# First batch of an FFT-mixing and SwiGLU kernel: its copies on VectorE, its loads and stores on other queues, and products of zeros on TensorE while it waits

## The chip, the cores and the metric

One core of a Trainium2 chip. The metric is the device time of one launch in microseconds (us); a time quoted for a kernel is the median of its runs. Engines in the profile: PE is TensorE (matrix products), PEld its weight loads, DVE is VectorE, ACT ScalarE, POOL GpSimd, SP the engine that only issues transfers. "ACTq", "POOLq" and "SPq" are the queues on which those engines issue transfers.

## The reference

```python
def _attn_ref(x, filt_r, filt_i):                 # x: 8 x 3008 x 256
    X = np.fft.rfft(x, axis=1)
    Y = X * (filt_r + 1j * filt_i)[None, :, :]
    return np.fft.irfft(Y, n=x.shape[1], axis=1).astype(np.float32)

def _moe_ref(x, w_gate, w_val, w_out):            # x: 24064 x 256; w: 256 x 1536, 1536 x 256
    g = x @ w_gate
    silu = g * (1.0 / (1.0 + np.exp(-g)))
    return (silu * (x @ w_val) @ w_out).astype(np.float32)
# reference: the first, reshaped to (8 * 3008, 256), then the second
```

The weights arrive as 64-bit numbers, and the kernel rounds them to float32 on the chip ("rounding" below).

## The kernel before

The transform over 3008 = 47 x 64 points is done in steps of products with tables. For each batch: the first step (`pa`) multiplies x by a 94x96 table and stores the result in DRAM (`d1`); the second step loads it back turned (`t`), multiplies by the table `tb` (2a), multiplies by the filter `f` on VectorE (`p`, `q`), adds `p` and `q` on GpSimd, multiplies by the inverse table (2b, `pc`), and stores `g` in DRAM (`d2`); the third step loads that (`t4`) and multiplies by the last table (`pd`), which gives `y`, the input of the feed-forward part. Batches 1 to 7 are woven into the feed-forward products of the batch before them. Batch 0 has nothing to hide behind: it stands alone at the start of the program, and it is what the change edits.

Several functions serve all batches; `self.b` is the number of the batch. Cuts are marked.

```python
def load_weights(j):                       # raw 64-bit weights, all on SP's queue
    if j < len(weights):
        raws[j] = rpool.tile([128, 2, 2, 128, 2], U32, name=f"raw_{j}", tag="raw", bufs=2)
        for i in range(2):
            nc.sync.dma_start(out=raws[j][:, i], in_=weights[j][0][:, i])

def round_weights(j):                      # VectorE, ScalarE, then GpSimd
    load_weights(j + 2)
    # ... (cut)

def load_tables(self, parts=3):            # class Spectral, batch 0 only
    # ... (cut)
    for i in range(parts):
        nc.scalar.dma_start(out=tb[:, ts(i, n)], in_=de_dram[:, ts(i, n)])
        for rows, view in filter_parts():  # 4 of them: f_r twice, f_i twice
            nc.scalar.dma_start(out=f[rows, ts(i, n), :], in_=view(n * i, n))

def stage1(self, u):                       # 16 steps a batch
    # ... (cut)
    p1 = spool0 if self.b == 0 and u % 2 else t1pool      # batch 0: 2 + 2 buffers
    t1 = p1.tile([NK, NV, C], FP32, name=f"t1_{self.b}_{u}", tag="t1", bufs=2)
    ps = fps.tile([128, NV, C], FP32, name=f"pa_{self.b}_{u}", tag="f")
    nc.tensor.matmul(out=ps[0:NK], lhsT=wf_t, rhs=self.x.pop(u), start=True, stop=True)
    nc.scalar.copy(out=t1, in_=ps[0:NK])
    queue = nc.scalar if self.b == 1 else nc.gpsimd
    queue.dma_start(out=self.d1_rows[:, ts(u, NV), :], in_=t1)

def stage2a(self, u):                      # 12 steps a batch; loads t on SP's queue
    # ... (loads and the two products into ps: cut)
    for h in (lo, hi):
        nc.vector.tensor_tensor(out=pt[h], in0=ps[h], in1=fr, op=ALU.mult)
    nc.vector.scalar_tensor_tensor(out=qt[lo], in0=ps[hi], scalar=-1.0, in1=fi,
                                   op0=ALU.mult, op1=ALU.mult)
    nc.vector.tensor_tensor(out=qt[hi], in0=ps[lo], in1=fi, op=ALU.mult)
    add(nc.gpsimd, pt, pt, qt)

def stage2b(self, u):
    # ... (two products into ps: cut)
    nc.scalar.copy(out=g, in_=ps)
    for p in range(2):
        queue = nc.scalar if self.b == 0 and p else nc.gpsimd
        queue.dma_start(out=..., in_=g[64 * p:64 * p + 64])

# the start of the program
for i in range(4):
    spec.load_x(i)                         # SP's queue
spec.load_tables()                         # ScalarE's queue
load_weights(0)
load_weights(1)
nc.sync.dma_start(out=wi_t, in_=wi_dram.ap())
for u in range(N_ONE):
    spec.stage1(u)
for _ in range(2):
    round_weights(todo.pop(0))
lag = 3
for u in range(N_TWO + lag):
    if u < N_TWO:
        spec.stage2a(u)
    if u >= lag:
        spec.stage2b(u - lag)
for i in range(2):
    spec.load_t4(0, i)
for step in range(4):
    spec.stage3(0, step)                   # pd and y
```

A scheduler orders the instructions of each engine; only those marked with `keep_in_program_order` are kept as written.

Of the kernel before, what the change touches and what calls it, by code (L numbers as in the profile page):

```python
# [49 lines left out]
NK = 4 * NS  # L50
# [53 lines left out]
def kernel(  # L104
# [10 lines left out]
    nc = tc.nc  # L115
# [3 lines left out]
    de_dram = nc.inline_tensor(de_host, name="de_tbl").ap()  # L119
# [23 lines left out]
    wv_t = cpool.tile([128, NJ, 7, 128], FP32)  # L143
# [5 lines left out]
    def filter_parts():  # L149

        for k, filt in enumerate((filt_r, filt_i)):
            for half in range(2):
                off, step = (0, 1) if half == 0 else (N1, -1)

                def view(s0, n, filt=filt, off=off, step=step):
                    return bass.AP(tensor=filt.tensor, offset=filt.offset + (off + step * s0) * C,
                                   ap=[[N1 * C, 32], [step * C, n], [1, C]])

                yield slice(64 * k + 32 * half, 64 * k + 32 * half + 32), view

    def add(eng, dst, a, b):
        eng.tensor_tensor(out=dst, in0=a, in1=b, op=ALU.add)  # L162

    def sub(eng, dst, a, b):
        eng.tensor_tensor(out=dst, in0=a, in1=b, op=ALU.subtract)  # L165
# [3 lines left out]
    def weight_parts():  # L169

        cols = [w.bitcast(U32).rearrange("(a p) (h j f two) -> j p h a f two",
                                         a=2, p=128, h=2, j=NJ, two=2)
                for w in (moe_w_gate, moe_w_val)]
        rows = moe_w_out.bitcast(U32).rearrange("(l j p) (c f two) -> j p l c f two",
                                                l=2, j=NJ, p=128, c=2, two=2)
        def hid(j):
            for w, dst in zip(cols, (wg_t, wv_t)):
                yield w[j], dst[:, j], True

        for q in range(NQB):  # L180
            for j in range(JB * q, JB * q + JB):
                yield from hid(j)
            for j in range(JB * q, JB * q + JB):
                yield rows[j], wo_t[:, j], False

    weights = list(weight_parts())
    raws = {}

    def load_weights(j):
        if j < len(weights):  # L190
            raws[j] = rpool.tile([128, 2, 2, 128, 2], U32, name=f"raw_{j}", tag="raw", bufs=2)
            for i in range(2):
                nc.sync.dma_start(out=raws[j][:, i], in_=weights[j][0][:, i])

    def round_weights(j):



        load_weights(j + 2)
        raw, (_, dst, left) = raws.pop(j), weights[j]  # L200
        low, high = raw[:, :, :, :, 0], raw[:, :, :, :, 1]
        pw = rpool.tile([128, 2, 2, 128], U32, name=f"pw_{j}", tag="pw")
        w = rpool.tile([128, 2, 2, 128], FP32, name=f"w_{j}", tag="w")
        man = w.bitcast(U32)
        v = nc.vector
        flat = "p a b f -> p (a b f)"
        flat2 = "p a b f two -> p (a b f) two"

        pin = tc.keep_in_program_order
        pin(v.tensor_scalar(out=man, in0=high, scalar1=0xFFFFF, scalar2=None,  # L210
                            op0=ALU.bitwise_and))
        pin(nc.scalar.activation(out=w, in_=man, func=AF.Copy, scale=2.0 ** -20, bias=1.0))
        pin(v.tensor_scalar(out=pw, in0=high, scalar1=20, scalar2=0x7FF,
                            op0=ALU.logical_shift_right, op1=ALU.bitwise_and))
        pin(nc.scalar.activation(out=pw, in_=pw, func=AF.Relu, bias=off_t))
        v.tensor_scalar(out=pw, in0=pw, scalar1=255.0, scalar2=2.0 ** 23,
                        op0=ALU.min, op1=ALU.mult)
        v.scalar_tensor_tensor(out=pw.rearrange(flat), in0=raw.rearrange(flat2)[:, :, 1],
                               scalar=0x80000000, in1=pw.rearrange(flat),
                               op0=ALU.bitwise_and, op1=ALU.bitwise_or)  # L220
        v.scalar_tensor_tensor(out=w.rearrange(flat), in0=raw.rearrange(flat2)[:, :, 0],
                               scalar=2.0 ** -52, in1=w.rearrange(flat),
                               op0=ALU.mult, op1=ALU.add)

        e = nc.gpsimd
        pin(e.tensor_tensor(out=dst[:, 0:4, :].rearrange("p (a b) f -> p a b f", b=2), in0=w,
                            in1=pw.bitcast(FP32), op=ALU.mult))
        if left:
            a11, a12, a21, a22, s1, s2, s4 = [dst[:, i] for i in range(7)]
            add(e, s1, a21, a22)  # L230
            sub(e, s2, s1, a11)
            sub(e, a21, a11, a21)
            sub(e, s4, a12, s2)
        else:
            b11, b12, b21, b22, t1, t2, t4 = [dst[:, i] for i in range(7)]
            sub(e, t1, b12, b11)
            sub(e, t2, b22, t1)
            sub(e, b12, b22, b12)
            sub(e, t4, b21, t2)
# [2 lines left out]

    def bank(kind, name):
        return wps.tile([128, 512], FP32, name=f"w{kind}_{name}", tag=kind)

    class Spectral:

# [47 lines left out]
        def load_tables(self, parts=3):  # L295

            tb = spool0.tile([128, NS, 2, 128], FP32, name="tb0")
            f = spool0.tile([128, NS, C], FP32, name="f0")
            n = NS // parts
            for i in range(parts):  # L300
                nc.scalar.dma_start(out=tb[:, ts(i, n)], in_=de_dram[:, ts(i, n)])
                for rows, view in filter_parts():
                    nc.scalar.dma_start(out=f[rows, ts(i, n), :], in_=view(n * i, n))
            for u in range(N_TWO):
                self.tb[u], self.f[u] = tb[:, ts(u, NV)], f[:, ts(u, NV)]

# [4 lines left out]
        def stage1(self, u):  # L311

            if self.b:
                for v in (0, 1, 2) if u == 0 else (u + 2,):
                    self.load_x(v)
            p1 = spool0 if self.b == 0 and u % 2 else t1pool
            t1 = p1.tile([NK, NV, C], FP32, name=f"t1_{self.b}_{u}", tag="t1", bufs=2)
            ps = fps.tile([128, NV, C], FP32, name=f"pa_{self.b}_{u}", tag="f")
            nc.tensor.matmul(out=ps[0:NK], lhsT=wf_t, rhs=self.x.pop(u), start=True, stop=True)  # L319
            nc.scalar.copy(out=t1, in_=ps[0:NK])  # L320
            queue = nc.scalar if self.b == 1 else nc.gpsimd
            queue.dma_start(out=self.d1_rows[:, ts(u, NV), :], in_=t1)

# [31 lines left out]
        def stage2b(self, u):  # L355

            pt, tb = self.p.pop(u), self.tb.pop(u)
            ps = fps.tile([128, NV, C], FP32, name=f"pc_{self.b}_{u}", tag="f")
            for i in range(NV):
                nc.tensor.matmul(out=ps[:, i, :], lhsT=tb[:, i, 1, :], rhs=pt[:, i, :],  # L360
                                 start=True, stop=True)
            p3 = spool0 if self.b == 0 and u % 2 else gpool
            g = p3.tile([128, NV, C], FP32, name=f"g_{self.b}_{u}", tag="g", bufs=2)
            nc.scalar.copy(out=g, in_=ps)
            for p in range(2):
                a0 = p * NS + NV * u
                queue = nc.scalar if self.b == 0 and p else nc.gpsimd
                queue.dma_start(out=self.d2[a0:a0 + NV].rearrange("s n c -> n s c"),
                                in_=g[64 * p:64 * p + 64])

# [151 lines left out]
    todo = list(range(len(weights)))  # L522
# [7 lines left out]
    with tc.tile_pool(name="start", bufs=1) as spool0:  # L530
        for i in range(4):
            spec.load_x(i)
        spec.load_tables()
        load_weights(0)
        load_weights(1)
        nc.sync.dma_start(out=wi_t, in_=wi_dram.ap())
        for u in range(N_ONE):
            spec.stage1(u)
        for _ in range(2):
            round_weights(todo.pop(0))  # L540
        lag = 3
        for u in range(N_TWO + lag):
            if u < N_TWO:
                spec.stage2a(u)
            if u >= lag:
                spec.stage2b(u - lag)
    for i in range(2):
        spec.load_t4(0, i)
    for step in range(4):
        spec.stage3(0, step)  # L550
    for _ in range(2):
        round_weights(todo.pop(0))
# [10 lines left out]
    for b in range(B):  # L563
# [26 lines left out]
        for i in range(NP):  # L590
            k, j = divmod(i, NJ)
# [47 lines left out]
```

## Time and profile before

| | before |
|---|---|
| time, median of the first three runs | 3150.79 us (3150.08 to 3152.27) |
| first product of the second step (2a) starts | 77.33 us |
| VectorE's work of the second step | 79.41 to 118.15 us |
| third step (pd) starts | 133.18 us |
| last subtraction of the third step on VectorE starts | 139.42 us |

The prediction below shows the emptiest and the fullest stretches of the start. These are the ones between (columns: stretch, length, then busy us and instructions of PE, PEld, DVE, ACT, POOL, granted clock, share of the 16 DMA engines, GB/s):

```profile
40.00:60.00 20.00, 15.71 (x18) 4.92 (x19) 0.00 (x0) 7.00 (x11) 5.31 (x10) 1.00 0.69 178
60.00:80.00 20.00, 11.48 (x17) 4.66 (x16) 3.34 (x6) 5.94 (x10) 6.37 (x11) 1.00 0.50 148
100.00:120.00 20.00, 10.17 (x28) 6.36 (x28) 15.09 (x22) 3.51 (x6) 9.42 (x11) 0.67 0.27 69
```

The first step runs from 40 to 70 us, on TensorE and ScalarE, after the loads; VectorE has almost nothing to do until 70 us. From 100 us to the end of its second step at 118.15 us VectorE, which should be the bound there, is busy for 15 us of 18. The list of its waits from 55 to 125 us (total us, times, longest) has a line for that:

```profile
DVE q L349 <- POOL p L162: 3.3, 3, 2.1
```

It waits for GpSimd's sums `p + q`, and GpSimd stands in order behind stores of `g` that it issues itself. Last, what the DMA engines moved from 20 to 40 us, while no product could run:

```profile
DMA packets 2062, 4.49 MB, mean 225 GB/s; under 512 B 201, under 2 KB 1701, under 8 KB 1701
```

### The profile page before, as it was taken

To read this page: it belongs to the slowest core of one execution; us is meant where nothing else is said; L and a number is where in the kernel's file an instruction comes from. 1 tells how busy PE (TensorE), PEld (TensorE's weight loads), DVE (VectorE), ACT (ScalarE), POOL (GpSimd) and SP (SyncE) were. 2 spreads that over 40 slices of the span, in tenths; PEclk is the share of its full clock that TensorE was granted. 3 is DMA by queue.
4 is the path that set the end of the run, shared out by engine and by line. 5 is a ranking of instruction groups with operands and counts; after the bars stand their busy time and mean duration, and the time that the engine had idled before them with its cause. 6 is when DMAs were issued, how large, how long until landed. Compare 5 with 4: busy or idle time off the path is not lost.

```text
span 3150.0 us, 41042 instructions
## 1 busy us (share of the span) xinstructions
PE 3042.9 (97%) x15488; PEld 2236.8 (71%) x15488; DVE 1461.6 (46%) x2331; ACT 1149.9 (37%) x2086; POOL 1409.8 (45%) x1634
## 2 busy tenths in 40 slices
PE   3689999999999999999999999999999999999999
PEld 1456777677777777777777677777777677777776
DVE  0665544345533445335543455434554445544443
ACT  1244333433334333433334433333333433333333
POOL 1475554345543345434444445434544345533333
PEclk9799999999999999999999999999999999999999
DMA  8432322213222223122222222221321212210000
GB/s 191 113 119 88 87 64 61 70 54 90 68 57 63 71 64 87 50 70 64 77 60 60 67 81 67 62 65 54 87 74 52 71 55 77 64 31 21 21 5 17
DMA packets 122481, 212.50 MB, mean 67 GB/s; under 512 B 23670, under 2 KB 68214, under 8 KB 121426
## 3 DMA queue, kind: packets, MB, share of 16 engines
q1 hardware_dynamic: 91388, 128.58, 14.8%
q0 software_dynamic: 25024, 70.29, 7.7%
q10 hardware_dynamic: 5872, 11.01, 1.5%
q8 instruction: 122, 2.00, 0.3%
q14 instruction: 75, 0.61, 0.1%
HBM read 134.81 MB, written 74.97 MB: 67 GB/s over the span
## 4 chain that ended last, share of the span: by engine, by line
PE 80%; POOL 8%; DVE 5%; issue 3%; DMA 2%; ACT 2%; SPq 0%; POOLq 0%; ACTq 0%; DVEq 0%
PE wA_v L419 15%; PE wA_g L419 15%; PE wA_o L483 7%; PE wE_v L419 7%; PE wE_g L419 7%; PE wE_o L483 7%; PE wF_o L483 4%; PE wF_g L419 4%; PE pd L380 4%; PE wF_v L419 3%; PE pa L319 3%; POOL o L162 3%; POOL h L165 3%; PE pc L360 3%; PE pb L340 2%
## 5 line engine op out<-in xcount | busy, mean ns | idle before, releaser
L419 PE MATMUL wA_v<-y,wv_t 128*128 128x376 f32 x1536 | 613.8, 481 | 8.6 <-ACT u_v L428 6.5
L419 PE MATMUL wA_g<-y,wg_t 128*128 128x376 f32 x1536 | 615.7, 483 | 0.9 <-ACT u_g L428 0.9
L165 POOL TENSOR_TENSOR h<-h 128x376 f32<-128x376 f32 x576 | 567.1, 985 | 28.8
L162 POOL TENSOR_TENSOR h<-h 128x376 f32<-128x376 f32 x192 | 189.0, 984 | 705.9 <-PE wE_v L419 387.7
L428 ACT COPY u_g<-wA_g 128x376 f32<-128x376 f32 x576 | 269.5, 468 | 587.3 <-PE wA_g L419 585.0
L419 PEld LDWEIGHTS wA_v<-y,wv_t 128*128 128x128 f32 x1536 | 290.7, 191 | 205.8 <-DVE h L441 15.8
L483 PEld LDWEIGHTS wA_o<-wo_t,h 128*128 128x128 f32 x3456 | 407.5, 193 | 16.5 <-issue 0.6
L483 PE MATMUL wA_o<-wo_t,h 128*128 128x128 f32 x3456 | 418.7, 276 | 0.0
L419 PEld LDWEIGHTS wA_g<-y,wg_t 128*128 128x128 f32 x1536 | 282.1, 191 | 167.2 <-issue 28.0
L446 ACT ACTIVATE s<-s 128x1128 f32<-128x1128 f32 x192 | 219.5, 1143 | 375.9 <-DVE s L162 375.9
L448 DVE TENSOR_TENSOR h<-s,h 128x1128 f32<-128x1128 f32 x192 | 256.3, 1335 | 123.4 <-ACT s L446 123.2
L419 PE MATMUL wE_v<-y,wv_t 128*128 128x376 f32 x768 | 307.9, 483 | 3.4 <-DVE h L162 3.4
L419 PE MATMUL wE_g<-y,wg_t 128*128 128x376 f32 x768 | 306.3, 481 | 1.8 <-DVE s L162 1.2
L428 ACT COPY u_v<-wA_v 128x376 f32<-128x376 f32 x576 | 272.2, 473 | 69.9 <-PE wA_v L419 66.0
L162 DVE TENSOR_TENSOR s<-u_g,wE_g 128x376 f32<-128x376 f32 x384 | 209.0, 544 | 176.8 <-ACT u_g L428 174.9
L483 PE MATMUL wE_o<-wo_t,h 128*128 128x128 f32 x2304 | 282.1, 277 | 7.5 <-DVE o L162 7.5
L162 DVE TENSOR_TENSOR s<-u_g,wF_g 128x376 f32<-128x376 f32 x192 | 104.5, 544 | 393.7 <-PE wF_g L419 375.4
L483 PE MATMUL wF_o<-wo_t,h 128*128 128x128 f32 x2304 | 278.6, 275 | 0.0
L483 PEld LDWEIGHTS wE_o<-wo_t,h 128*128 128x128 f32 x2304 | 267.7, 192 | 14.1 <-DVE o L162 13.6
L483 PEld LDWEIGHTS wF_o<-wo_t,h 128*128 128x128 f32 x2304 | 267.8, 192 | 0.3
L162 DVE TENSOR_TENSOR h<-u_v,wE_v 128x376 f32<-128x376 f32 x384 | 209.1, 545 | 28.1 <-ACT u_v L428 5.1
L419 PEld LDWEIGHTS wE_v<-y,wv_t 128*128 128x128 f32 x768 | 146.3, 191 | 102.1 <-DVE h L162 5.1
(82 smaller groups left out, 3222.7 us busy)
## 6 DMA issues: line engine op xcount, KB each, us to landing
t<-d SPq DMA_DIRECT2D x192, 128.0 KB
t<-d SPq DMA_DIRECT2D x64, 384.0 KB
d<-g POOLq DMA_DIRECT2D x180, 128.0 KB, 2.8
d<-t POOLq DMA_DIRECT2D x112, 192.0 KB, 2.4
tb<-de_tbl SPq DMA_DIRECT2D x84, 256.0 KB
x<-in_x_dram SPq DMA_DIRECT2D x112, 160.0 KB
out_dram<-o POOLq DMA_DIRECT2D x128, 128.0 KB, 2.0
f<-in_filt_r_dram SPq DMA_DIRECT2D x168, 64.0 KB
```

What stands on the lines that cost most here:

```text
L162: eng.tensor_tensor(out=dst, in0=a, in1=b, op=ALU.add)
L165: eng.tensor_tensor(out=dst, in0=a, in1=b, op=ALU.subtract)
L319: nc.tensor.matmul(out=ps[0:NK], lhsT=wf_t, rhs=self.x.pop(u), start=True, stop=True)
L340: nc.tensor.matmul(out=ps[:, i, :], lhsT=self.tb[u][:, i, 0, :], rhs=t2[:, i, :], start=True, stop=True)
L360: nc.tensor.matmul(out=ps[:, i, :], lhsT=tb[:, i, 1, :], rhs=pt[:, i, :], start=True, stop=True)
L380: nc.tensor.matmul(out=psv[:, n, :], lhsT=self.t4[k, i][:, n, ts(cb, 128)], rhs=wi_t, start=True, stop=True)
L419: nc.tensor.matmul(out=bk[z][kind], lhsT=wt[z][:, j, LEFT[p], :], rhs=y[:, RIGHT[p], :], start=start, stop=True, skip_group_check=True)
L428: nc.scalar.copy(out=u[(1, 6, 7).index(p)], in_=bk[z]["A"])
L446: nc.scalar.activation(out=s[:, 0:3], in_=s[:, 0:3], func=AF.Silu)
L448: nc.vector.tensor_tensor(out=h[:, 0:3], in0=s[:, 0:3], in1=h[:, 0:3], op=ALU.mult)
L483: nc.tensor.matmul(out=bk[kind][:, t, :], lhsT=hs[i][:, HID[p], t0:t0 + 128], rhs=wo_t[:, JB * q + i, WO[p], :], start=start and t == 0 an ...
```

## The change

Its intent: let the first step follow x as it lands, instead of after all loads; take issue work off GpSimd in the second step; and keep TensorE's clock up through the waits with products of zeros ("fillers"). The core of the diff:

```diff
-    def load_weights(j):
+    def load_weights(j, queue=nc.sync):
...
-    def round_weights(j):
-        load_weights(j + 2)
+    def round_weights(j, following=True):
+        if following:
+            load_weights(j + 2)
...
+    def warm(count, width=4):
+        for i in range(count):
+            ps = bank("F", "idle")[:, 0:128 * width]
+            tc.keep_in_program_order(nc.tensor.matmul(
+                out=ps, lhsT=wv_t[:, 0, 0, :],
+                rhs=wv_t[:, 0, 0:width, :].rearrange("p i f -> p (i f)"), start=True, stop=True))
...  (load_tables)
-                nc.scalar.dma_start(out=tb[:, ts(i, n)], in_=de_dram[:, ts(i, n)])
+                nc.sync.dma_start(out=tb[:, ts(i, n)], in_=de_dram[:, ts(i, n)])
                 for rows, view in filter_parts():
-                    nc.scalar.dma_start(out=f[rows, ts(i, n), :], in_=view(n * i, n))
+                    queue = nc.scalar if rows.start >= 64 else nc.sync
+                    queue.dma_start(out=f[rows, ts(i, n), :], in_=view(n * i, n))
...  (stage1)
-            nc.scalar.copy(out=t1, in_=ps[0:NK])
+            if self.b:
+                nc.scalar.copy(out=t1, in_=ps[0:NK])
+            else:
+                nc.vector.tensor_copy(out=t1, in_=ps[0:NK])
...  (stage2b)
-                queue = nc.scalar if self.b == 0 and p else nc.gpsimd
+                queue = nc.gpsimd if self.b else nc.scalar
...  (the start of the program)
-        load_weights(0)
-        load_weights(1)
+        load_weights(0, nc.scalar)
+        load_weights(1, nc.scalar)
         nc.sync.dma_start(out=wi_t, in_=wi_dram.ap())
+        nc.vector.memset(wv_t[:, 0], 0.0)
+        warm(5)
         for u in range(N_ONE):
             spec.stage1(u)
+            warm(1, 2)
+        warm(6)
         for _ in range(2):
-            round_weights(todo.pop(0))
+            round_weights(todo.pop(0), False)
...  (after the second step)
+    for j in (2, 3):
+        load_weights(j)
     for i in range(2):
         spec.load_t4(0, i)
+    warm(9)
```

So raw weights 2 and 3 are now loaded after the second step, in program order, and not at the first two roundings.

More of the change, by code (lines that the diff above doesn't have):

```diff
@@ L192, in load_weights @@
             for i in range(2):
-                nc.sync.dma_start(out=raws[j][:, i], in_=weights[j][0][:, i])
-    def round_weights(j):
-        load_weights(j + 2)
+                ins = queue.dma_start(out=raws[j][:, i], in_=weights[j][0][:, i])
+                if j in (2, 3):
+                    tc.keep_in_program_order(ins)
+    def round_weights(j, following=True):
+        if following:
+            load_weights(j + 2)
         raw, (_, dst, left) = raws.pop(j), weights[j]
```

## The prediction

> **What bounds the kernel now.** I read the page first, then the table by stretches, then the chain of work over the first 145 us, then the waits there, and last the timeline and the DMA queues of the same stretch.
>
> ```profile
> PE 3042.9 (97%) x15488; PEld 2236.8 (71%) x15488; DVE 1461.6 (46%) x2331; ACT 1149.9 (37%) x2086; POOL 1409.8 (45%) x1634
> PE   3689999999999999999999999999999999999999
> ```
>
> From 280 us on TensorE is never idle, so only the start can give anything. (A slice is 78.75 us: the 3 and the 6 are the first 157 us.) The change edits the first batch only; with line and buffer numbers removed, the instructions of TensorE are the same in both kernels from about the 220th of 7782 on, and those of the other engines likewise after the start. I take the rest as shifted in time, not altered. By stretches (columns: PE, PEld, DVE, ACT, POOL busy, granted clock, DMA share, GB/s):
>
> ```profile
> 0.00:20.00 20.00, 3.98 (x4) 0.79 (x4) 0.06 (x1) 0.00 (x0) 0.20 (x4) 1.00 0.95 210
> 20.00:40.00 20.00, 0.00 (x0) 0.00 (x0) 0.76 (x2) 0.00 (x0) 0.00 (x0) 1.00 1.06 225
> 80.00:100.00 20.00, 14.14 (x56) 10.86 (x54) 18.91 (x30) 2.34 (x4) 11.84 (x15) 1.00 0.65 182
> 120.00:140.00 20.00, 10.60 (x40) 9.38 (x41) 1.31 (x2) 2.81 (x4) 4.44 (x6) 0.50 0.34 83
> ```
>
> For 40 us nothing computes and the DMA engines are full; then VectorE is the bound (18.91 of 20); then nothing is, in a tail at half the clock. The chain of waits says why (start, length, what):
>
> ```profile
> 11.36 18.38 DMA tb<-de_tbl
> 30.20 10.08 DMA raw<-in_moe_w_val_dram
> 40.66 1.28 ACT L320
> 42.84 7.88 DMA d<-t
> 51.43 17.40 PE pa L319 x20
> ...
> 73.70 3.50 DMA t<-d
> 77.33 2.06 PE wA_b L340 x4
> ...
> 133.18 7.11 PE pd L380 x32
> ```
>
> The first step's products (pa) had data at 11 us, but their copies stand on ScalarE behind 15 table loads that it issues itself, and the last of those gets into its queue at 40.6 us:
>
> ```profile
> ACT L320 <- DMA raw<-in_moe_w_val_dram: 40.7, 1, 40.7
> PE pa L319 <- ACT t L320: 28.1, 2, 26.4
> PE pd L380 <- DMA t<-d: 7.7, 1, 7.7
> ```
>
> After that pa runs at 1.71 us a step (timeline: 7.04 us for four steps). In the second batch two of its instructions take 0.88 to 1.02 us, so it runs at half speed here, although the granted clock of the page reads 1.00.
>
> **What the Trainium skill says.** "TensorE: Matmul & The Clock Gate", Part 1, states that the array runs at half clock until activity of about 3.4 us has been seen, and falls back after an idle window of that length. The trace agrees on the fall (pd 7.11 us for 32 instructions at 133 us, 1.76 for 16 at 229 us). It does not agree on the rise: 17.4 us of gapless pa products stay at half speed, while the full 128x128 products from 77 us on speed up within about 5 us. "TensorE: Matmul & The Clock Gate", Part 1, "Architectural detail", calls ScalarE a strict FIFO: the 40.7 us wait above is that. "DMA: Bandwidth & Descriptors", "Rules for kernel authors", says that spreading transfers over issuing engines gives no bandwidth, only issue time, as all run on the same 16 engines. The trace of 0 to 40 us agrees, the two queues' shares adding to one whole:
>
> ```profile
> q10 hardware_dynamic: 1583, 4.54, 51.8%
> q1 hardware_dynamic: 1795, 4.16, 48.9%
> ```
>
> **The change part by part.**
>
> *Start of the second step (2a).* The copies go to VectorE, which has nothing to do, so the first step can follow x as it lands. VectorE's 64x512 operations from PSUM take 0.69 us (timeline), so a copy of 96x512 costs about that, 16 of them 11 us beside the loads. But the transfers remain: x, tables and two raw weights together are 10.3 MB, which at the measured 218 GB/s is 47 us, and the trace shows the queues full until about 48 us. The first step's stores, 16 of 192 KB, ran alone from 50 to 70 us at 36 to 40% of the engines, so they need 10 us of all engines. In the old kernel these follow the loads; now they mix with them. As loads and stores share the engines, 47 + 10 = 57 us is the earliest that everything is done. The loads of the second step (t<-d) stand on the SP queue behind x, all of tb and half of f, the longest of the three queues, so I expect them at about 57 us, the first landing 3.5 us later (as at 73.70). First 2a product: 60.5 instead of 77.3: **16.8 us**. The five zero products before are about 7 us and end before x; the half-width ones between (0.43 us each at full speed) and the six after lie in the wait. They matter to the clock only.
>
> *Second step on VectorE.* From 79.41 to 118.15 it took 38.7 us. Its period per step where nothing else interferes is 2.83 us (p starts at 86.62, 89.44, 92.27, 95.10), so 12 steps need 33.9. The rest is 1.6 us of rounding the second weight and 3.3 us of waits for GpSimd's sums, which stood in order behind GpSimd's own stores of g. Rounding now falls in the wait before 2a, and all g stores go to ScalarE (a copy of 0.58 and two issues of about 0.6 us are under 2.83). So 38.7 becomes 34.1: **4.6 us**.
>
> *Tail.* From VectorE's end at 118.15 to pd at 133.18 are 15.0 us. Now: sum 1.3, two products 1.1 to 2.1, copy 0.6, issues 0.6, landing 2.6, t4 load 3.8, some 0.4 between: 10.4 to 11.4. Against it stand the nine filler products (by now with real weights, as the zeros are overwritten): 0.86 us each at full speed, 1.71 cold. If TensorE has cooled as before, two to four are slow and the nine take 9.4 to 11 us, while the transfers they cover take about 8. I count 11.8 us from VectorE's end to pd: **3.2 us**.
>
> *Third step.* pd at full speed is 2 x 1.76 = 3.5 instead of 7.1 us: **3.6 us**. Behind it, the products at 140 us run at 1.25 us a pair instead of 0.63, but they soon wait for rounded weights (weight product on TensorE at 152.9 waits for GpSimd), a chain that starts with VectorE after pd. So little more: **0.5 us**.
>
> Sum: 16.8 + 4.6 + 3.2 + 3.6 + 0.5 = 28.7 us. 3150.8 - 28.7 = **3122 us**.
>
> **The rivals.** *The tables do not bind; the first step does.* SP's packets are larger, so its queue may get more than its share and finish early; t<-d would then go as soon as the last store has landed, near 50 us. That the author placed only six filler products (5.2 us) after the first step speaks for it: about a store and a load. Against: all queues seem saturated until the sum is through. It would give 7 us more: 3115. *The queue order turns the gain into a new wait.* The SP queue alone, with few transfers admitted at a time, does not fill the engines, or stores under full load take as long as the one at 42.84 (7.88 us), four buffers at a time, which stretches the first step. 2a would start near 68: 3130. From 40 to 45 us one queue alone held 98% of the engines, which speaks against the first half. *The fillers are too long.* Cold, nine take 15.4 us, delaying pd by 4 to 5 us against my count: 3127. *The gain is swallowed later*, because from 140 to 245 us weight rounding, not TensorE, sets the pace (GpSimd busy 17.89 of 20 us from 160 on). But that work starts relative to pd and its loads wait on buffers, not on a fixed time, so it moves along; if half were lost, 3136.
>
> **Range and chances.** The start of 2a is the widest term (52 to 67 us), the tail and the fillers plus or minus 3. I predict **3122 us**, 3113 to 3132 eight times in ten. Two per cent is 63 us. To win it the whole start would have to shrink from 140 to 77 us, less than the 57 us of transfers and the 34 us of VectorE work in series; to lose it needs a fault that nothing here hints at. Faster 0.01, same 0.98, slower 0.01.
>
> **What would show each step.** In the changed profile: the first pa copy on VectorE before 15 us; DMA shares near 1 to about 57 us with all three queues in it; the first 2a product at 60.5; VectorE's second step 34 us long, without waits for GpSimd; pd beginning 11 to 12 us after it and lasting 3.5 us; the same spacing from pd to the steady state, about 29 us earlier. I am wrong if 2a starts at 52 or 68, if the fillers end well after t4 has landed, or if the lead at 150 us is not the lead at the end.

## The result, and the profile after

| | before | after | earlier by |
|---|---|---|---|
| time, median of four runs | 3151.23 us | 3118.31 us | 32.9 us |
| first 2a product | 77.33 | 55.09 | 22.2 us |
| VectorE's second step | 79.41 to 118.15 (38.7 long) | 57.07 to 90.95 (33.9 long) | 27.2 us at its end |
| pd starts | 133.18 | 102.99 | 30.2 us |
| last subtraction of the third step | 139.42 | 108.43 | 31.0 us |
| span of the profiled run | 3150.0 | 3116.7 | 33.3 us |

The ratio of the times is 0.9898, with a 95% interval of 0.9881 to 0.9915. By the 2% rule the two kernels count as the same; the interval still excludes 1.

The page of the kernel after, totals and TensorE's slices:

```profile
PE 3056.4 (98%) x15560; PEld 2240.5 (72%) x15560; DVE 1476.5 (47%) x2348; ACT 1140.3 (37%) x2070; POOL 1405.8 (45%) x1622
PE   7789999999999999999999999999999999999999
```

TensorE is busier by 13.5 us than before, and the program is shorter: the fillers fill idle time. The first three slices (78 us each) read 7, 7, 8 where they read 3, 6, 8. A busy TensorE in the first slice is therefore no sign of progress here. The stretches say more (columns as before):

```profile
0.00:20.00 20.00, 15.50 (x34) 6.97 (x34) 3.61 (x6) 1.28 (x1) 2.44 (x8) 1.00 0.96 200
20.00:40.00 20.00, 13.69 (x33) 6.48 (x33) 6.18 (x9) 0.00 (x0) 4.10 (x8) 0.83 1.03 331
40.00:60.00 20.00, 16.24 (x35) 8.87 (x36) 10.54 (x18) 2.56 (x4) 9.03 (x15) 0.74 0.69 217
60.00:80.00 20.00, 15.29 (x63) 10.83 (x61) 19.50 (x29) 4.04 (x7) 8.98 (x8) 1.00 0.64 172
```

VectorE works from the first stretch on (the copies), and from 60 to 80 us it is the bound of the second step, at 19.50 of 20. The DMA engines are full to 40 us as before, yet they moved 331 GB/s where they had moved 225. The chain of waits (start, length, what) shows what sets each part:

```profile
15.21 10.54 DMA d<-t
...
33.70 7.52 DMA d<-t
...
45.09 6.15 DMA d<-t
...
55.34 2.42 DMA t<-d
...
92.44 2.08 PE pc L376 x4
94.51 8.64 PE wF_idle L254 x18
103.15 0.88 PE pd L396 x8
104.06 0.82 ACT y L407
104.92 0.90 PE wA_g L435 x2
105.82 1.77 PE pd L396 x16
```

Where table loads and a copy on ScalarE stood, there are now the landings of the first step's stores (`d<-t`, 6 to 10 us each): eight of the sixteen copies waited for one of the four buffers to come free, 18.0 us in total. After 94 us the fillers (`wF_idle`) stand on the path, and within pd a product of the feed-forward part (`wA_g`) that waited 0.91 us for a copy on ScalarE. SP's waits up to 60 us name what the second step's loads waited for:

```profile
SPq L304 <- DMA d<-t: 7.8, 3, 6.3
```

The loads of `t` were issued at 51.38 us, when the last store had landed. The DMA engines from 20 to 40 us, the counterpart of the line with the 4.49 MB:

```profile
DMA packets 2316, 6.62 MB, mean 331 GB/s; under 512 B 334, under 2 KB 1415, under 8 KB 1872
q1 hardware_dynamic: 863, 3.93, 60.0%
q0 software_dynamic: 611, 1.87, 29.4%
q10 hardware_dynamic: 842, 0.81, 14.1%
```

Queue q0 is GpSimd's and carries the first step's stores; q1 is SP's and q10 ScalarE's, and both carry loads alone in this stretch. The loads make 3.93 + 0.81 = 4.74 MB, no less than the 4.49 MB of before. The 1.87 MB of stores came on top. Over all of the first 48 us the change moved 10.37 MB of loads and 2.70 MB of stores, the kernel before 10.39 and 0.12.

### The profile page after: what moved, and what is told of

Its sections match the earlier page's. It is cut to its first block, busy times and chain, and to the rows that moved or that the text cites. A ratio compares the mean times of both kernels' runs of the same rounds, so it can differ in the third digit from the quotient of the medians.

```text
span 3116.7 us, 41163 instructions
## 1 busy us (share of the span) xinstructions
PE 3056.4 (98%) x15560; PEld 2240.5 (72%) x15560; DVE 1476.5 (47%) x2348; ACT 1140.3 (37%) x2070; POOL 1405.8 (45%) x1622
## 4 chain that ended last, share of the span: by engine, by line
PE 80%; POOL 7%; DVE 6%; issue 3%; DMA 2%; ACT 2%; SPq 0%; POOLq 0%; ACTq 0%; DVEq 0%
PE wA_v L435 15%; PE wA_g L435 15%; PE wA_o L499 7%; PE wE_v L435 7%; PE wE_g L435 7%; PE wE_o L499 7%; PE wF_o L499 4%; PE wF_g L435 4%; PE pd L396 3%; PE wF_v L435 3%; POOL o L162 3%; PE pa L332 3%; POOL h L165 3%; PE pc L376 2%; PE pb L356 2%
## 5 line engine op out<-in xcount | busy, mean ns | idle before, releaser
L162 POOL TENSOR_TENSOR p<-p,q 128x512 f32<-128x512 f32 x96 | 121.6, 1266 | 226.4 <-DVE q L367 226.4
```

The costliest lines, as they stand in the source:

```text
L162: eng.tensor_tensor(out=dst, in0=a, in1=b, op=ALU.add)
```

## The experiments

Theories before the first run. Main theory: the gain is the copies (the first step runs beside the loads), then the queues of `g`, and the fillers give next to nothing. Rival: the fillers' clock gives several us. On the start of 2a there were two more: the landing of the stores through four buffers sets it, or the amount of transfers queued ahead of the loads of `t` does. The kernels ran in three groups, each with its own runs of the kernel before, whose medians were 3148.96 us (the first four kernels below), 3151.91 (the next four) and 3151.28 (the last four); so ratios are compared across groups, and times within one; each group ran on another chip.

### 1. The change without its fillers

```diff
-        warm(5)
-            warm(1, 2)
-        warm(6)
-    warm(9)
```

> The changed kernel without any filler product. Theory A (the second step starts when the last store of the first step has landed; the first step is paced by those landings through four buffers of t; the fillers only serve the clock of the third step): first 2a product at 55 to 57 us, VectorE's second step 34 us, pd at half clock, 7 us long; total 3119 to 3123. Rival C (the fillers carry a good part of the gain, by keeping the first and second steps at full clock): 2a at 60 or later, or a longer second step; total 3126 or more.

Measured: 3119.88 us, ratio 0.9908 (0.9893 to 0.9923), against 0.9898 for the change. 2a starts at 53.73. The third step, from the timeline (start, length, what, and in brackets how long TensorE had been idle and for what):

```profile
101.10 7.11 PE L396 MATMUL pd<-wi_t,t 96*128 96x94 f32 x32 [7.82 <-DMA t<-d]
```

pd is cold and 7.11 us long, as in the kernel before, but starts 11.4 us after VectorE's last product (89.71), sooner than in the change, where the fillers hold it for 12.0. From that last product to the last subtraction it is 17.6 us without fillers and 17.5 with them. What the clock gives, the overshoot of the fillers takes: each is under 1 us in these traces. The rival, that the fillers carry several us, fell with the total.

### 2. The copies alone

The kernel before, with only this of the change:

```diff
-            nc.scalar.copy(out=t1, in_=ps[0:NK])
+            if self.b:
+                nc.scalar.copy(out=t1, in_=ps[0:NK])
+            else:
+                nc.vector.tensor_copy(out=t1, in_=ps[0:NK])
```

> The kernel before, with only the copies of the first step moved to VectorE; all queues as before, no fillers. Theory A: stores mix with the loads at almost no cost, so the last store lands near 50 us and 2a starts at 52 to 57 us; GpSimd's own stores of g still hold up its sums, pd is cold; total 3125 to 3132. Rival B (loads and stores share one capacity, as the prediction had it): 2a at 60 us or later, total 3134 or more.

Measured: 3135.70 us, ratio 0.9958 (0.9943 to 0.9973), somewhat slower than expected. 2a starts at 55.25, so this one line brings the whole gain at that point. But the second step on VectorE then takes 43.4 us (57.34 to 100.76), longer than before. The timeline has both roundings' operations between its products from 68 to 78 us, and the old waits for GpSimd are still there (VectorE's waits):

```profile
DVE q L352 <- POOL p L162: 3.4, 3, 1.9
```

I had not foreseen this: the earlier start moved the second step into the rounding. ScalarE's waits say why: it has a part in each rounding, and it still issues all table loads itself, the last of them at 60.2 us.

```profile
ACT L212 <- DMA t<-d: 60.2, 1, 60.2
```

In the change ScalarE is through with its loads at 18.2 us, both weights are rounded before the second step, and GpSimd has no stores of `g` to issue there; of these, only the stores were tested by themselves (experiment 3).

This kernel also gives the cleanest look at loads and stores side by side, since its loads stand in the queues of the kernel before. From 20 to 40 us:

```profile
q1 hardware_dynamic: 1339, 2.57, 43.6%
q10 hardware_dynamic: 742, 1.84, 33.2%
q0 software_dynamic: 505, 1.56, 27.8%
```

In the kernel before, q1 and q10 moved 2.58 and 1.91 MB there, in 60.7% and 45.5% of the engines' time. So nearly the same loads, in packets of nearly the same size, took 77% of that time instead of 106%, and the stores filled the rest. A full share did not mean that the engines could move no more. By 48 us 9.89 MB of loads were through, against 10.39 before; the difference is the last two table loads, which ScalarE issued only from 55.8 us on.

### 3. Half of the stores of g back on GpSimd

```diff
-                queue = nc.gpsimd if self.b else nc.scalar
+                queue = nc.scalar if self.b == 0 and p else nc.gpsimd
```

> The changed kernel with half of the stores of g back on GpSimd. Theory A: 2a at 55 us as in the changed kernel; VectorE's second step 36 to 38 us instead of 34 because it waits for GpSimd's sums, and 2 to 4 us more from its end to pd; total 3122 to 3126. Rival (the queue of these stores does not matter, what slowed the second step before was the rounding in it): 34 us and total 3118.

Measured: 3122.75 us, ratio 0.9918 (0.9903 to 0.9932). The second step takes 35.8 us instead of 33.9, and the way from its end to pd 14.6 instead of 12.0. VectorE's waits for GpSimd are there again:

```profile
DVE q L365 <- POOL p L162: 1.9, 1, 1.9
```

So this part of the change is worth about 4.5 us up to pd (1.9 in the second step, 2.6 behind it) in the traces.

### 4. Eight buffers for the first step's results

For batch 0, every second pair of `t1` tiles comes from two pools that are still idle then, which makes eight buffers where there were four:

```diff
+            if self.b == 0 and u % 4 > 1:
+                p1, tag = ((fpool, "f"), (gpool, "g"))[u % 2]
+                t1 = p1.tile([128, NV, C], FP32, name=f"t1_{self.b}_{u}", tag=tag, bufs=2)[0:NK]
+            else:
                 p1 = spool0 if self.b == 0 and u % 2 else t1pool
```

> The changed kernel with eight buffers instead of four for the copies of the first step (the four new ones borrowed from tiles that are not yet in use). Theory A: VectorE no longer waits for stores to land, the first step ends 4 to 8 us earlier, 2a at 47 to 52 us, total 3110 to 3116. Rival B (the transfers are the limit, buffers only decide where the wait shows): 2a within 1.5 us of 55, total 3117 to 3120.

Measured: 3116.80 us, ratio 0.9896 (0.9879 to 0.9912), the same as the change. The last copy of the first step starts at 33.83 instead of 44.11, ten us earlier, and 2a does not move. First SP's timeline, then TensorE's, then the queue from 40 to 48 us:

```profile
43.10 28.79 SPq L304 DMA_DIRECT2D t<-d  x24
```

```profile
55.62 2.08 PE L360 MATMUL wA_b<-t,tb 128*128 128x256 f32 x4 [16.25 <-DMA t<-d]
```

```profile
q1 hardware_dynamic: 562, 1.96, 99.5%
```

The loads of `t` are issued at 43.10, eight us earlier, but land as late as before: they stand in SP's queue behind 7.87 MB of x and tables, of which 7.80 at most had moved by 50 us, and the queue fills the DMA engines until 52 us (106.6% from 48 to 52). The theory that the landing through four buffers alone sets the start fell.

### 5. The copies back on ScalarE, the rest of the change kept

```diff
-            if self.b:
-                nc.scalar.copy(out=t1, in_=ps[0:NK])
-            else:
-                nc.vector.tensor_copy(out=t1, in_=ps[0:NK])
+            nc.scalar.copy(out=t1, in_=ps[0:NK])
```

> The changed kernel with the copies of the first step back on ScalarE; queues and fillers stay. ScalarE now issues 14 transfers instead of 15 before its first copy and was free of them at 18.2 us in the changed kernel. Theory D (two things limit the start of 2a at the same place: the landing of the first step's stores, and the sum of loads and stores through the DMA engines, done near 51 us either way): the first step begins near 19 us and ends a few us later than the 44 of the changed kernel, 2a at 55 to 58 us, total 3118 to 3122. Rival (the move of the copies is what carries the gain): 2a at 62 us or later, total 3126 or more.

Measured: 3123.25 us, ratio 0.9906 (0.9892 to 0.9921). 2a starts at 60.02, between the two expectations. ScalarE's waits:

```profile
ACT L333 <- DMA raw<-in_moe_w_gate_dram: 20.1, 1, 20.1
ACT t L333 <- DMA d<-t: 18.0, 10, 5.2
```

With the tables moved to SP's queue, ScalarE has only ten loads to issue (the 14 of the expectation was a miscount) and starts its first copy at 21.43 us instead of 41.95. So most of the blocking goes away by the queue part of the change alone; VectorE is worth another 2 to 5 us at this point (2a of the change started at 55.09 us in one profile and at 57.58 in another), because it can start with the first x. Experiments 2 and 5 overlap: either part alone removes most of the same wait, and their gains do not add.

### 6. Two thirds of the tables behind the first loads of t

To test the queue limit of experiment 4: eight buffers as there, and parts 1 and 2 of `tb` and of `f`'s real half (3.1 MB) are issued on SP's queue after the loads of `t` for steps 0 to 2, and of steps 3 to 5. Those transfers and the products of batch 0's second step are kept in program order.

```diff
             for i in range(parts):
-                nc.sync.dma_start(out=tb[:, ts(i, n)], ...)          # and f_r on SP
+                part(i, late=False)            # part 0 of tb and f_r; all of f_i, on ScalarE
...  (stage2a)
+            if self.b == 0 and u == 0:
+                self.late_part(1)              # after load_two(0..2)
             self.load_two(u + ahead)
+            if self.b == 0 and u == 2:
+                self.late_part(2)              # after load_two(5)
```

> The eight-buffer kernel with the second and third part of tb and of the real filter (3.1 MB) moved behind the first and fourth loads of the second step on the SP queue, and the product order of the second step fixed. Theory D: with both limits taken away, the loads of the second step are no longer behind 3.1 MB of tables, 2a at 42 to 47 us, total 3106 to 3113 (some of the 10 us may go again in the second step, where rounding of one weight now falls in it and the late tables compete). Rival (the first step itself, by x, cannot be done before 50 us): 2a at 52 us or later, total 3116 or more.

Measured: 3112.47 us, ratio 0.9874 (0.9860 to 0.9889): the fastest kernel. TensorE's timeline, the first product of 2a and pd:

```profile
43.29 1.10 PE L378 MATMUL wA_b<-t,tb 128*128 128x256 f32 x4 [2.05 <-DMA t<-d]
...
95.69 3.98 PE L422 MATMUL pd<-wi_t,t 96*128 96x94 f32 x32
```

2a comes 11.8 us earlier than in the change, and its first products are at full speed, since fillers run up to 2 us ahead of them. By the ratios some 7.5 us of those 11.8 reach the end (0.9898 less 0.9874, of 3151; the two intervals overlap a little): the second step on VectorE now takes 39.2 us instead of 33.9, because the rounding of the second weight falls into it and loads of `t` stand behind late tables. pd has no feed-forward product in its middle and lasts 3.98 us. The fixed order of the products came with the late tables and was not tested alone.

### 7. The late tables with the change's four buffers

Experiment 6 without the edit of experiment 4.

```diff
-            if self.b == 0 and u % 4 > 1:
-                p1, tag = ((fpool, "f"), (gpool, "g"))[u % 2]
-                t1 = p1.tile([128, NV, C], FP32, name=f"t1_{self.b}_{u}", tag=tag, bufs=2)[0:NK]
-            else:
                 p1 = spool0 if self.b == 0 and u % 2 else t1pool
```

> The same late tables with the changed kernel's four buffers. Theory D: the stores land faster once the tables no longer load beside them, but still pace the first step: 2a at 46 to 52 us, total 3110 to 3117. If four buffers alone were the limit of the changed kernel, 2a stays at 54 to 56 us.

Measured: 3117.12 us, ratio 0.9890 (0.9874 to 0.9907), just past the slow edge of what was expected. 2a starts at 46.97. Together with experiments 4 and 6: more buffers alone move 2a by nothing, fewer tables ahead of it by 8 us, both by 12. In the change the two limits end within a few us of each other (the stores at 51, the tables at about 48), so more buffers alone show nothing. Moving the tables acts on both: the last store lands at 43.4 us here, since it has fewer loads beside it (median landing 4.7 us from 20 to 50 us, where the change has about 7).

### 8. No fillers between the first step's products

```diff
             spec.stage1(u)
-            warm(1, 2)
```

> The changed kernel without the sixteen half-width fillers between the products of the first step. If narrow products (94 rows, 96 columns) do not hold the clock by themselves, the first step's products fall to 0.85 us each after a few us although TensorE has work; if they do, they stay at 0.43 us each while they follow each other closely. Theory D: 2a at 53 to 56 us in either case, total 3116 to 3121.

3117.37 us; 2a at 53.80. It was run for the clock. TensorE's timeline of this kernel, and below it that of the change:

```profile
25.91 7.45 PE L332 MATMUL pa<-wg_t,wf_t 94*96 94x512 f32 x8
```

```profile
27.92 1.05 PE L332 MATMUL pa<-wg_t,wf_t 94*96 94x512 f32 x2
```

A step is two instructions. Without the fillers between, four steps take 7.45 us without a gap, 1.86 each; with them one takes 1.05. Here products of 94 x 96 did not lift the clock by themselves in 7.45 us without a gap; with the full 128x128 fillers between, it was up. But as the first step waits for transfers, nothing comes of it.

### 9. Both roundings ahead of the second step

Experiment 6, with VectorE's roundings of the first two weights and batch 0's filter products kept in program order.

```diff
+        fix = pin if j < 2 else (lambda ins: ins)         # on the three free rounding operations
...  (stage2a)
+            fix = tc.keep_in_program_order if self.b == 0 else (lambda ins: ins)   # on p and q
```

> The late-tables kernel with eight buffers, and VectorE's order fixed so that both first weights are rounded before the second step. If the 39 us of its second step were 34 us of work plus the rounding (3 to 4 us) plus waits for late loads (2 us): 36 to 37 us now, total 3108 to 3112. If the late tables are what stretches it: still 38 us or more, total 3112 or more.

Measured: 3112.59 us, ratio 0.9879 (0.9864 to 0.9893), against 3119.61 for the change in the same group; of its four runs (3111.41, 3112.35, 3112.82, 3117.48) the profiled one is the slowest, and the other three lie below every run of the change. So kernels with the late tables came out some 7 us ahead of the change twice, though the intervals of the ratios overlap a little each time. Of the two expectations for the second step, 36 to 37 us failed and the other, 38 us or more, held: it took 42.2 (45.30 to 87.52). The rounding is out of it, and instead VectorE stands still twice for over 4 us, at 53.7 and at 66.4 us. TensorE's waits say for what:

```profile
PE wA_b L379 <- DMA t<-d: 12.5, 2, 6.8
```

Loads of `t` behind the late tables. So the loads behind the late tables, not the rounding, cost most of what the early start won; an order that feeds both is left open.

### 10 and 11. The change again, and again without fillers, in one group

No edit, and the edit of experiment 1, to compare the two with the same runs of the kernel before.

> The changed kernel itself, to be compared with the next on one chip. 3116 to 3121.

> The changed kernel without any filler, again. If the fillers are worth nothing: within 2 us of the changed kernel of this call. If they are worth the 3.6 us that the prediction gave to a fast third step: 3 to 5 us longer.

Measured: 3119.61 us, ratio 0.9897 (0.9880 to 0.9913) for the change, and 3120.48, ratio 0.9901 (0.9886 to 0.9916), without fillers. The difference is 0.9 us, well within the spread of one kernel's runs (3116.98 to 3122.22). From VectorE's last product to the last subtraction: 17.1 and 17.5 us. And the changed kernel, built again without an edit, started 2a at 57.58 here and at 55.09 in its first profile, again as the last store had landed (`t` was issued at 54.09): readings of that one point differ by some 2.5 us from run to run.

### 12. Without the nine last fillers alone

```diff
-    warm(9)
```

> The changed kernel without the nine fillers ahead of the third step. The scheduler then leaves the four groups of pd together. Fillers worth nothing: pd starts about 1 to 2 us earlier after VectorE's end, lasts 7.1 us at half clock, and the last y comes at the same distance from VectorE's end (17 to 18 us) as in the changed kernel; total within 2 us. Fillers useful: that distance grows by 3 us, total 3120 or more.

Measured: 3122.33 us, ratio 0.9906 (0.9891 to 0.9921). The distance from VectorE's last product to the last subtraction is 17.7 us, 0.6 more than with them in this group and 0.2 more than in the first profile. The median is 2.7 us over that of the change in the same group, but the runs overlap (3119.29 to 3124.84 against 3116.98 to 3122.22), and the kernel without any fillers lies between; I take nothing from it but that the nine are worth little at most.

## Why the prediction was right

The total was right: 3122 us (3113 to 3132) predicted, 3118.31 measured, and the class too. Its five terms, with the traces of before and after:

| term | predicted gain | measured gain |
|---|---|---|
| start of 2a | 16.8 us | 22.2 us |
| second step on VectorE | 4.6 | 4.9 (38.7 to 33.9), 0.1 more on its start |
| tail to pd | 3.2 | 3.0 (15.0 to 12.0) |
| third step, to its last subtraction | 3.6 | 0.8 (6.24 to 5.44) |
| later | 0.5 | 2.3 |
| sum | 28.7 | 33.3 (spans) |

**Start of 2a: the mechanism right, the size wrong.** The copies on VectorE and the transfers as the limit were as described, and all loads were indeed through at about 47 to 48 us. The term that failed is "47 + 10 = 57 us is the earliest that everything is done". It treated full DMA engines as a fixed 218 GB/s and added the stores' time to the loads'. Measured, the loads were hardly slowed by the stores (4.74 against 4.49 MB from 20 to 40 us, 10.37 against 10.39 by 48 us), and everything was done at 51 us: from 50.5 to 52.8 us the engines moved 1 GB/s, where the prediction had them full to about 57. (Twelve of the sixteen stores, not all of them, ran from 50 to 70 us, in 38% of the engines' time; scaled to sixteen, the 10 us stands.) `t` was issued at 51.38, as the last store landed, and its first product came 3.7 us later; the 3.5 us for that was right. In the second profile of the change 2a gained 19.8 us, so the surplus over the 16.8 is 3 to 5 us. This is the first rival of the prediction, "near 50 us", whose 3115 us brackets the result from the other side. Its reason, that SP's queue gets more than its share and finishes early, is half true at most: the queue took 60.0% of the engines from 20 to 40 us, but had the most to load and was the last one through, at about 48 us.

**Second step and tail: right, and for the reasons given.** Experiment 3 puts the old waits back by undoing the one line that was named. The count of 11.8 us to pd met 12.0, and 11.7 in the second profile; the fillers end with it (103.15 us in the chain). Without any fillers it is 11.3 to 11.4.

**Third step: the mechanism was blocked.** "pd at full speed is 3.5" was true of the clock and not of the stretch: it took 5.75 us (102.99 to 108.74), because the scheduler put a feed-forward product, waiting for a copy, into its middle. Where that product stood elsewhere (experiment 6), pd took 3.98. I had looked at the durations and not at the order of TensorE's instructions there. That the nine fillers would cost more time than the clock returns was argued under "the fillers are too long", with 4 to 5 us; measured, they cost about 0.5 us and return about 0.8 (17.5 and 17.1 us to the last subtraction with them, 17.6 and 17.5 without).

**Later: the lead was not swallowed.** It was 31.0 us at the last subtraction, 31.5 at the first rounding product on GpSimd behind it (144.62 before, 113.16 after), and 33.3 at the end. The fourth rival, half of it lost, fell. The 2.3 us over are no more than one kernel's runs differ by, and I did not look for their cause.

The surplus at the start (5.4 us) and on the later term (1.8), less the 2.8 us short in the third step, makes the 4.6 us that the prediction was below the gain in spans (the other two terms change it by 0.2 us). Part of the good total is thus two errors in opposite directions.

What the prediction did not see at all: the fillers, the largest part of the text of the change, are worth about 1 us or nothing (experiments 1, 10 and 11), and the copies alone, without the queues, lost part of what they won (experiment 2: 22.1 us at 2a, 4.7 of them gone again in the second step, and at the end 13 us by its ratio, 0.0042 of 3149).

## What to carry to other kernels

When an engine's copies stand behind loads that the same engine issues, move either; the other then adds less (here 17 us of the 22 at 2a came without the move of the copies, in experiment 5). A full share of the DMA engines is not a fixed rate: before adding up bytes, look whether stores and loads ran in the same time, and for what else stands ahead in the same queue. And an earlier start is worth only what the next stage can take: here 12 us gained at 2a with late tables became about 7 at the end, and keeping an engine's clock up with fillers was worth nothing where the wait behind it was for a transfer.

## What the Trainium skill lacked or had wrong

- "TensorE: Matmul & The Clock Gate", Part 1, gives a budget of about 3.4 us of busy time for the rise of the clock. Here gapless products of 94x96 stay at half speed for 17.4 us (the kernel before) and for 7.45 us (experiment 8, whose first step at 8.55 us still ran at full speed), while the 128x128 products of 2a in the change start cold at 55.09 and are fast from 58.53 us, 3.4 us later, as the page has it. It does not say there that the size of the product matters; which of its sizes does was not tested.
- The same page, Part 1, "Seeing it yourself", warns that the clock events of a trace are not to be fully trusted, and this agrees: the granted clock reads 1.00 from 0 to 20 us in experiment 1, where five steps of pa take 8.82 us, twice their time at full speed. The length of one product was the safer reading.
- "DMA: Bandwidth & Descriptors", "Rules for kernel authors", says that more issuing engines give no bandwidth for loads, and this agrees: SP's queue nearly alone moved 1.96 MB in 8 us (245 GB/s, experiment 4), two queues together 225 GB/s. It does not say that stores beside the loads can come on top: at a full share in both, 225 GB/s for loads alone and 299 (experiment 2) or 331 (the change) with stores among them. The cause is not settled: in experiment 2 the packets of the loads hardly differ, but the stores also bring a third queue.
- The same page, "Anatomy of one DMA — SWDGE (gpsimd) path", calls the fixed cost of about 2 us constant and adds only a term for the bytes; for 192 KB an estimate by its formula is 2.45 us. The 192 KB stores issued by GpSimd landed in 2.3 us with the engines partly free, as the page has it, but in 6 to 10.5 us with all of them full, for which the formula has no term; with four buffers that landing time was on the path.
